# Block attention and a gated product: seven products in 76 of the 80 blocked units, the scans of v at unit ends, and the copy and block sums ahead of tanh in eight units

## The chip, the cores and the metric

One core of a Trainium2 chip. The metric is the device time of one execution in microseconds (us). The engines are named as the profile names them: PE (TensorE matmuls), PEld (its weight loads), DVE (VectorE), ACT (ScalarE), POOL (GpSimd) and SP (SyncE, which issues nearly all DMAs).

## The reference

```python
# attention within chunks of 64 rows, 8 batches x 8 heads x 576 rows, head_dim 64
scores = scale * np.matmul(q_c, k_c.transpose(0, 1, 2, 4, 3))
attn = np.exp(scores - np.max(scores, axis=-1, keepdims=True))
attn = attn / (np.sum(attn, axis=-1, keepdims=True) + 1e-09)
out = np.matmul(attn, v_c)
# its result, as x of 4608 rows by 512, goes through
h = x @ w_in          # 512 x 2048
g = h - np.tanh(h)
return (g @ w_out).astype(np.float32)   # 2048 x 512
```

## The kernel before

The 4608 rows are nine groups of 512. Groups 0 and 1 are computed in a plain way while weights are prepared; groups 2 to 8 go through the class `Fast`. There a group is two halves (b = 0, 1), and a half is eight units (j = 0 to 7). A unit takes two of the sixteen column blocks of `w_in` (j and j + 8) for 256 rows. Its first product gives four 128x128 blocks of h in PSUM (`ph`, two buffers); tanh and a subtraction follow; sums of blocks of the result go, as seven 128x128 operands in two f16 parts each (`gh`, `gl`), through the second product. All matmuls of this stage are f16, three for each operand pair (high*high, low*high, high*low).

From group SEVEN = 4 on x is kept in 2x2 blocks ("blocked"), 5 groups, 10 halves, 80 units. A unit's first product is made there in one of two ways. **Plain** (`gemm1`, L691): 24 matmuls of 256 columns. **Seven products** (`seven`, L706): 42 matmuls of 128 columns, in two parts, P5, P4, P1, P6 (24 matmuls) and P2, P7, P3 (18). Between the two parts ACT copies three blocks of `ph` to SBUF (`kept_back`, L711) and DVE adds them up (`joined`, L715 and L716); the second part accumulates on what `joined` wrote and waits for it. After it DVE adds once more (`completed`, L721). `in_seven` (L955) chooses: before, plain are all units with j = 3, j = 0 to 2 of group 4's first half, and j = 6, 7 of the last half: 15 plain, 65 seven.

The seven products need combined weights (`sums`). They are made once, one j at a time, by `Half.seven` in six POOL operations, two ACT copies and two DVE subtractions (L556), cut into seven steps, which `make_in` puts among the units of groups 2 and 3; they are stored to DRAM (`kept`) and read back two units before use into three rotating places (`load`, L854), except j = 6 and 7, which stay.

The order on every engine is the order of the code in `run`. For unit s of the blocked stage: PE the first part of s; loads; `closing` (DVE `completed` of s - 1); extra work of slot 0; ACT tanh of s - 1 (L725); `kept_back` and `joined` of s; `shrink` of s - 1 (DVE L732, then three POOL lines L733 to L735); `split` of s - 2 (ACT L744, DVE L745); PE the second product of s - 3 (L764), and where that ends a half the output arithmetic of `finish` (three ACT, three POOL, five DVE L777); PE the second part of s; extra work of slot 1. So PE's second part of s stands behind DVE's `joined` of s, and the first part of s behind `shrink` of s - 2, which frees its buffer.

The extra work is the attention of the next group, which `beside` places in the units by hand (key 2 * unit + slot). For each half it falls on the same j:

- j = 3: slot 0 PE weights times values, slot 1 `blocks`: twice ACT L425, L426 and DVE L427, the second round behind the first one's L427
- j = 4: slot 0 `differences` (POOL) and the scan of v, `halves` (DVE L311; in first halves also L313); slot 1 PE scores, more differences, and in second halves six tiny DVE operations of `power_of` (L578 to L583)
- j = 5: slot 0 DVE `largest` (L363); j = 6: slot 0 `shifted`; j = 7: `totals`; j = 0: `divided`; j = 1: the transposes; j = 2: POOL `split_low`

For group 4 itself this lies among the plain units of group 3; its second scan stands at slot 0 of unit 5 there, and PE's `spread` (L290), which reads it, at slot 1 of that unit.

Of the kernel before, what the change touches and what calls it, by code (L numbers as in the profile page):

```python
# [31 lines left out]
FC = DFF // P  # L32
# [3 lines left out]
NG = len(SIZES)  # L36
# [23 lines left out]
def attn_ffn_kernel(ctx: ExitStack, tc: tile.TileContext, qE, kE, vE, qL, kL, vL, w_in, w_out, out):  # L60
# [604 lines left out]
    class Fast:  # L665
# [146 lines left out]
        def run(self, at, before):  # L812
# [50 lines left out]
            for unit in units:  # L863
                s = unit["s"]
                unit["x"] = self.x = xs[unit["g"], unit["b"]]
                if unit["seven"]:
                    unit["sums"] = unit.get("sums") or resident[unit["j"]]
                    unit["ph"] = ps_h.tile([P, 4, P], F32, name="ph")
                    self.seven(unit, ("P5", "P4", "P1", "P6"))
                else:  # L870
                    self.gemm1(unit["b"], unit["j"])
                    unit["ph"] = self.ph
                while loads and loads[0]["s"] <= s + 2:
                    load()
                if pending:
                    closing(pending)
                for f in at.pop(o + 2 * s, []):
                    f()
                t = self.tanh() if pending else None
                if unit["seven"]:  # L880
                    self.kept_back(unit)
                    self.joined(unit)
                last, self.ready = self.ready, None
                if pending:
                    self.ph = pending["ph"]
                    self.shrink(pending["b"], pending["j"], t=t)
                last, self.ready = self.ready, last
                self.split()
                self.ready = last
                if self.stores:  # L890
                    self.stores[0] -= 1
                    if not self.stores[0]:
                        self.stores.pop()()
                        self.stores = None
                if len(self.queue) > (s >= (SEVEN - FAST) * n + 2) and unit is not units[-1]:
                    self.gemm2()
                if unit["seven"]:
                    self.seven(unit, ("P2", "P7", "P3"))
                for f in at.pop(o + 2 * s + 1, []):
                    f()  # L900
                pending = unit
# [51 lines left out]
            store(nc.scalar, 0, left)  # L953

    def in_seven(g, b, j):  # L955
        return j != 3 and (g, b, j // 4) != (SEVEN, 0, 0) and (g, b, j // 6) != (NG - 1, 1, 1)

    def beside(att, at, g):

        o = 2 * FC * (g - FAST)  # L960

        def put(unit, part, f, *args):
            at[o + 2 * unit + part].append(lambda: f(*args))

        put(-4, 0, att.halves, g, 0)
        late = g == SEVEN
        put(4 + late, 0, att.halves, g, 1)
        put(12, 1, lambda: powers.update({g: half.power_of(g)}))
        for b, u in enumerate((3, 11)):
            first = g == SEVEN and not b  # L970
            put(u + 1 + first, 1, att.scores, g, b)
            put(u + 2 + first, 0, att.largest, g, b)
            put(u + 3, 0, att.shifted, g, b)
            put(u + 3, 1, att.exponent, g, b)
            put(u + 4, 0, att.totals, g, b)
            put(u + 5, 0, att.divided, g, b)
            put(u + 5, 1, att.high, g, b)
            put(u + 6, 0, att.transpose, g, b)
            put(u + 6, not first, att.split_high, g, b)
            put(u + 7 - first, first, att.split_low, g, b)  # L980
            put(u + 8, 0, att.values, g, b)
            put(u + 8, 1, att.blocks, g, b)
            put(u + 9, 0, att.differences, g, b, 0)
            put(u + 9, 1, att.differences, g, b, 1)
            put(u + 10, 1, att.rounded_high, g, b, 1)
            put(u + 10, 1, att.rounded_low, g, b, 1)
            put(u + 11, 1, att.rounded_high, g, b, 0)
            put(u + 11, 1, att.rounded_low, g, b, 0)
            if g + 1 < NG:
                for i in range(2):  # L990
                    p = FIRST[g + 1] + 2 * b + i, 2 * b + i
                    put(u + 2 + i, 1, att.load, *p, "q")
                    put(u + 4 + i, 1, att.load, *p, "k")
                    put(u + 7, 1, att.load, *p, "v")
        put(6 - late, late, att.spread, g)
        put(6 - late, 1, att.greatest, g)
# [245 lines left out]

    def make_in(i, j):
        if j not in made_in:
            made_in[j] = half.seven(j, temporary[i % 2] if i else stream[2], stream[i % 2] if j < FC // 2 - 1 else temporary[1], j == FC // 2 - 1)
        next(made_in[j])

    o = 2 * FC * (SEVEN - FAST)
    at[o - 23].append(rooms)
    at[o - 15].append(more_rooms)  # L1250
    steps = [[29 * i // 4 - 22 + k for k in (0, 1, 2, 4, 5, 6, 7)] for i in range(FC // 2 - 1)]
    wanted = [j for j in range(FC // 2) if any(in_seven(g, b, j) for g in range(SEVEN, NG) for b in range(2))]
    for i, j in enumerate(wanted):
        for k in steps[i]:
# [83 lines left out]
```

## Time and profile before

| what | value |
|---|---|
| median of 3 runs | 785.83 us (785.73 to 786.14) |
| the profiled execution's own time | 786.32 us |
| its span, first to last instruction | 784.5 us |
| granted TensorE clock | 1.00 |
| PE busy | 770.5 us, 98% |
| DVE busy | 635.0 us, 81% |
| POOL busy | 502.3 us, 64% |
| ACT busy | 479.5 us, 61% |
| blocked stage, first seven-product unit to end | 396.35 to 784.5 us |

The profile gives for each engine when an instruction began and how long it lasted; a row of the timeline merges neighbours of one kind (x24), and the bracket at its end says how long the engine had stood idle and which instruction ended that. A matmul's end is modelled, so PE's pace is read from starts.

### The profile page before, as it was taken

The numbers are of one execution on the slowest core, as the hardware profiler recorded it, in microseconds if no ns is written. First come the engines' busy times: TensorE is split into PE (matmuls) and PEld (weight loads), VectorE is DVE, ScalarE is ACT, GpSimd is POOL, SyncE is SP. The second block draws the span as 40 slices with busy tenths as digits, with TensorE's granted clock in tenths as the row PEclk, the third lists the DMA queues.
The fourth block names the chain that finished last, engine by engine and source line by source line (L and its number), as shares of the span: only waits on it lengthen the run. The fifth ranks groups of instructions, "written<-read, shape, count | busy, mean of one in ns | idle before, by whom it ended". The sixth has DMA issues, their size and how long they took to land. (4 is left out here: it accounts for less than half of the span.)

```text
span 784.5 us, 23249 instructions
## 1 busy us (share of the span) xinstructions
PE 770.5 (98%) x9839; PEld 662.8 (84%) x9839; DVE 635.0 (81%) x1021; ACT 479.5 (61%) x787; POOL 502.3 (64%) x572
## 2 busy tenths in 40 slices
PE   8999999999999999999999999999999999999997
PEld 4878886666788888888899998999999989999996
DVE  5896998888698887786878887888888888787565
ACT  5877988566466455364556565747565656566443
POOL 1100002586678889689677777777867786878763
PEclk9999999999999999999999999999999999999999
DMA  9854441210233333133363535353534442424110
GB/s 347 315 196 164 162 162 53 81 28 2 81 81 95 82 109 96 42 82 122 82 217 72 198 61 186 83 181 91 164 108 145 125 139 60 131 58 135 55 55 28
DMA packets 74600, 91.68 MB, mean 117 GB/s; under 512 B 34560, under 2 KB 41728, under 8 KB 74496
## 3 DMA queue, kind: packets, MB, share of 16 engines
q1 hardware_dynamic: 74064, 89.55, 37.1%
q8 instruction: 77, 1.26, 0.7%
q10 hardware_dynamic: 432, 0.66, 0.2%
q14 instruction: 27, 0.22, 0.1%
HBM read 70.25 MB, written 12.58 MB: 106 GB/s over the span
## 5 line engine op out<-in xcount | busy, mean ns | idle before, releaser
L733 POOL TENSOR_TENSOR xl<-xl 128x256 f32<-128x256 f32 x111 | 146.5, 1320 | 113.3 <-DVE xl L732 101.4
L725 ACT ACTIVATE t<-ph,sig 128x512 f32<-128x512 f32 x112 | 77.0, 687 | 153.5 <-DVE ph L721 123.3
L691 PE MATMUL ph<-xh,wh 128*128 128x256 f16 x1068 | 123.7, 273 | 1.5 <-DVE xl L732 1.5
L691 PEld LDWEIGHTS <-wh 128*128 128x128 f16 x1068 | 103.4, 98 | 14.3 <-issue 2.2
L732 DVE SCALAR_TENSOR_TENSOR xl<-ph,sig,t 128x512 f32<-128x512 f32 x112 | 83.3, 744 | 27.4 <-ACT t L725 27.2
L706 PE MATMUL ph<-xh,wl 128*128 128x128 f16 x1344 | 97.8, 219 | 0.0
L706 PE MATMUL ph<-xh,wh 128*128 128x128 f16 x1332 | 95.7, 219 | 0.9 <-DVE ph L716 0.8
L764 PEld LDWEIGHTS <-gh 128*128 128x128 f16 x924 | 88.0, 98 | 10.1 <-issue 0.4
L764 PEld LDWEIGHTS <-wl 128*128 128x128 f16 x882 | 85.2, 98 | 9.6
L745 DVE SCALAR_TENSOR_TENSOR gl<-xl,to_g,gh 128x896 f16<-128x896 f32 x68 | 85.4, 1255 | 9.4 <-ACT gh L744 9.4
L764 PE MATMUL po<-wl,gh 128*128 128x256 f16 x610 | 87.7, 273 | 0.2 <-DVE wl L777 0.2
L706 PEld LDWEIGHTS <-wh 128*128 128x128 f16 x1332 | 81.7, 98 | 4.9 <-DVE ph L716 3.6
L735 POOL TENSOR_TENSOR xl<-xl 128x256 f32<-128x256 f32 x111 | 82.7, 745 | 0.0
L764 PE MATMUL po<-wl,wl 128*128 128x256 f16 x549 | 82.1, 273 | 0.0
L706 PEld LDWEIGHTS <-wl 128*128 128x128 f16 x1344 | 81.0, 98 | 0.8
L744 ACT ACTIVATE gh<-xl,to_g 128x896 f16<-128x896 f32 x68 | 71.0, 1045 | 15.3 <-POOL xl L735 14.9
L734 POOL TENSOR_TENSOR xl<-xl 128x128 f32<-128x128 f32 x111 | 67.5, 608 | 0.0
L764 PE MATMUL po<-wh,wl 128*128 128x256 f16 x333 | 59.7, 273 | 0.0
L605 PE MATMUL ph<-xh,wh 128*128 128x512 f16 (+2 forms) x252 | 59.3, 378 | 0.4 <-ACT xh L269 0.4
L745 DVE SCALAR_TENSOR_TENSOR wl<-xl,to_g,wl 128x896 f16<-128x896 f32 x44 | 55.1, 1253 | 5.1 <-ACT wl L744 5.0
L744 ACT ACTIVATE wl<-xl,to_g 128x896 f16<-128x896 f32 x44 | 45.9, 1043 | 15.3 <-POOL xl L735 14.2
L636 PE MATMUL po<-wh,gh 128*128 128x512 f32 x128 | 52.8, 415 | 0.0
(231 smaller groups left out, 1602.2 us busy)
## 6 DMA issues: line engine op xcount, KB each, us to landing
wl<-kept SPq DMA_DIRECT2D x96, 256.0 KB, 3.8
raw<-w_in SPq DMA_DIRECT2D x16, 512.0 KB, 3.8
raw<-w_out SPq DMA_DIRECT2D x16, 512.0 KB, 5.3
xl<-qL SPq DMA_DIRECT2D x28, 256.0 KB, 3.5
rawv<-vL SPq DMA_DIRECT2D x28, 256.0 KB, 3.0
rawk<-kL SPq DMA_DIRECT2D x28, 256.0 KB, 4.6
out<-wl SPq DMA_DIRECT2D x55, 128.0 KB, 2.6
kept<-wl SPq DMA_DIRECT2D x12, 256.0 KB, 2.2
```

The costliest lines, as they stand in the source:

```text
L605: nc.tensor.matmul(ph, lhsT=w[:, kc * P:(kc + 1) * P], rhs=x[b][:, kc, cols], start=(k == 0), stop=(k == 3 * KC - 1))
L636: nc.tensor.matmul(self.po[t], lhsT=gg[a][:, ts], rhs=wt[fc][1][b], start=(fc == 0 and a == b == 0), stop=(fc == FC - 1 and a == 1))
L691: nc.tensor.matmul(self.ph[:, 1 - f::2, :], lhsT=half_w[fc][:, w, kc * P:(kc + 1) * P], rhs=rhs, start=(k == 0), stop=(k == 3 * KC - 1))
L706: nc.tensor.matmul(ph[:, o], lhsT=a[:, w, i * P:(i + 1) * P], rhs=x[v][:, m, i * P:(i + 1) * P], start=(n == "P5" and k == i == 0), stop=( ...
L725: nc.scalar.activation(t, self.ph, AF.Tanh, scale=self.powers[0])
L732: nc.vector.scalar_tensor_tensor(out=u[:, :4], in0=self.ph, scalar=sig, in1=t, op0=ALU.mult, op1=ALU.subtract)
L733: engine.tensor_add(u[:, 4:6], u[:, 1:3], u[:, 0:4:3])
L734: engine.tensor_add(u[:, 6], u[:, 1], u[:, 2])
L735: engine.tensor_sub(u[:, 0:4:3], u[:, 0:2], u[:, 2:4])
L744: nc.scalar.activation(gh, u, AF.Copy, scale=powers[1])
L745: nc.vector.scalar_tensor_tensor(out=gl, in0=u, scalar=powers[1], in1=gh, op0=ALU.mult, op1=ALU.subtract)
L764: nc.tensor.matmul(place[m], lhsT=part[:, self.SUM[m]], rhs=w[m][:, o], start=first, stop=(last and part is gl), skip_group_check=True)
```

## The change

Five edits:

1. `in_seven`: plain remain j = 0, 1 of group 4's first half and j = 6, 7 of the last half. Eleven units change to seven products: j = 2 and 3 of (4, 0) and j = 3 of the nine other halves.
2. An eighth product (j = 3) is therefore made: the steps start every 6.5 half-units instead of 7.25, for eight j's, and the temporaries alternate the other way round.
3. `halves` (scan of v) goes from slot 0 to slot 1 of its unit.
4. Group 4's own second scan goes from slot 0 of unit 5 to slot 1 of unit 2.
5. In units with j = 4, groups 4 to 7, `kept_back` and `joined` come before `closing` and tanh of the unit before.

```diff
+                early = unit["seven"] and unit["j"] == FC // 4 and unit["g"] < NG - 1
+                if early:
+                    self.kept_back(unit)
+                    self.joined(unit)
                 if pending:
                     closing(pending)
                 for f in at.pop(o + 2 * s, []):
                     f()
                 t = self.tanh() if pending else None
-                if unit["seven"]:
+                if unit["seven"] and not early:
                     self.kept_back(unit)
                     self.joined(unit)
...
     def in_seven(g, b, j):
-        return j != 3 and (g, b, j // 4) != (SEVEN, 0, 0) and (g, b, j // 6) != (NG - 1, 1, 1)
+        return (g, b, j // 2) != (SEVEN, 0, 0) and (g, b, j // 6) != (NG - 1, 1, 1)
...
-        put(-4, 0, att.halves, g, 0)
+        put(-4, 1, att.halves, g, 0)
         late = g == SEVEN
-        put(4 + late, 0, att.halves, g, 1)
+        put(4 - 2 * late, 1, att.halves, g, 1)
...
-            made_in[j] = half.seven(j, temporary[i % 2] if i else stream[2], stream[i % 2] if j < FC // 2 - 1 else temporary[1], j == FC // 2 - 1)
+            made_in[j] = half.seven(j, temporary[1 - i % 2] if i else stream[2], stream[i % 2] if j < FC // 2 - 1 else temporary[1], j == FC // 2 - 1)
...
-    steps = [[29 * i // 4 - 22 + k for k in (0, 1, 2, 4, 5, 6, 7)] for i in range(FC // 2 - 1)]
+    steps = [[(13 * i - 43) // 2 + k for k in (0, 1, 2, 4, 5, 6, 7)] for i in range(FC // 2)]
```

## Rows read from the trace of the kernel before

**Rows 1.** The page's first part: span, then busy time and share of each engine.

```profile
span 784.5 us, 23249 instructions
PE 770.5 (98%) x9839; PEld 662.8 (84%) x9839; DVE 635.0 (81%) x1021; ACT 479.5 (61%) x787; POOL 502.3 (64%) x572
```

**Rows 2.** Busy time by stretch: PE, PEld, DVE, ACT, POOL; group 3, then one blocked unit.

```profile
267.00:390.00 123.00, 118.46 (x1502) 105.03 (x1500) 95.37 (x115) 62.08 (x85) 102.29 (x114) 1.00 0.30 88
...
445.88:450.51 4.63, 4.63 (x65) 4.40 (x63) 4.51 (x8) 3.07 (x6) 3.87 (x5) 1.00 1.01 351
```

**Rows 3.** Timeline of PE, units j = 3 to 5 of half (4, 1): start, duration, instruction.

```profile
430.28 2.78 PE L691 MATMUL ph<-xh,wh 128*128 128x256 f16 x24
...
436.21 0.50 PE L706 MATMUL ph<-xh,wl 128*128 128x128 f16 x6
...
437.55 0.38 PE L764 MATMUL po<-wh,wl 128*128 128x256 f16 x2
...
440.03 0.51 PE L706 MATMUL ph<-xh,wh 128*128 128x128 f16 x6
...
442.23 0.51 PE L706 MATMUL ph<-xh,wl 128*128 128x128 f16 x6
...
445.88 0.50 PE L706 MATMUL ph<-xh,wh 128*128 128x128 f16 x6
```

**Rows 4.** Timeline of PE: a wait in group 3, one in (4, 0), one in (5, 0).

```profile
320.40 0.49 PE L290 MATMUL po<-ident,sums 128*128 128x128 f32 x2 [1.33 <-DVE sums L313]
...
385.51 0.71 PE L691 MATMUL ph<-xh,wh 128*128 128x256 f16 x5 [1.52 <-DVE xl L732]
...
480.24 0.51 PE L706 MATMUL ph<-xh,wh 128*128 128x128 f16 x6 [0.28 <-DVE ph L716]
```

**Rows 5.** Timeline of DVE over the same units of (4, 1); last, one row of (5, 0).

```profile
432.18 0.42 DVE L721 TENSOR_TENSOR ph<-ph,t 128x256 f32<-128x256 f32 x1
433.36 0.75 DVE L732 SCALAR_TENSOR_TENSOR xl<-ph,sig,t 128x512 f32<-128x512 f32 x1 [0.76 <-ACT t L725]
434.29 1.57 DVE L745 SCALAR_TENSOR_TENSOR wl<-xl,to_g,wl 128x896 f16<-128x896 f32 x1 [0.18 <-ACT wl L744]
435.79 0.68 DVE L427 SCALAR_TENSOR_TENSOR xh<-psa,xh 128x512 f16<-128x512 f32 x1
437.62 0.69 DVE L427 SCALAR_TENSOR_TENSOR xh<-psa,xh 128x512 f16<-128x512 f32 x1 [1.15 <-ACT wh L426]
438.22 1.21 DVE L311 TENSOR_REDUCE v<-rawv 128x1 f32<-128x1024 f32 x1
439.35 0.29 DVE L715 TENSOR_TENSOR ph<-ph,t 128x128 f32<-128x128 f32 x1
439.67 0.30 DVE L716 TENSOR_TENSOR ph<-ph,t 128x128 f32<-128x128 f32 x1
439.88 0.74 DVE L732 SCALAR_TENSOR_TENSOR xl<-ph,sig,t 128x512 f32<-128x512 f32 x1
440.54 1.14 DVE L745 SCALAR_TENSOR_TENSOR gl<-xl,to_g,gh 128x896 f16<-128x896 f32 x1
...
443.82 1.22 DVE L363 TENSOR_REDUCE mx<-psa 128x16 f32<-128x1024 f32 x1
...
445.43 0.30 DVE L716 TENSOR_TENSOR ph<-ph,t 128x128 f32<-128x128 f32 x1
...
479.43 0.21 DVE L313 TENSOR_SCALAR sums<-v 128x1 f32<-128x1 f32 x1
```

**Rows 6.** Timeline of ACT (tanh, split, copy) and of POOL in the same units.

```profile
432.64 0.69 ACT L725 ACTIVATE t<-ph,sig 128x512 f32<-128x512 f32 x1 [2.73 <-DVE ph L721]
433.23 1.03 ACT L744 ACTIVATE wl<-xl,to_g 128x896 f16<-128x896 f32 x1
...
438.04 0.49 ACT L711 COPY t<-ph 128x384 f32<-128x384 f32 x1
...
440.70 1.56 POOL L733 TENSOR_TENSOR xl<-xl 128x256 f32<-128x256 f32 x1 [1.50 <-DVE xl L732]
```

## The prediction, made before the changed kernel ran

> **What bounds the kernel now.** I read the page first: PE is busy 98% of the span at full clock, DVE 81% [rows 1]. So fewer columns on PE should be time won, if nothing else becomes late. The second view is the busy time by stretch: in an ordinary blocked unit of 4.63 us DVE is busy 4.51 [rows 2]. The share of 81% hides that: DVE has spare time only at j = 0 to 2 and in waits. The third view is PE's timeline: its starts give its pace and the few places where it waits [rows 3, 4]. The last are DVE's and ACT's timelines over units j = 3 to 5, where the change acts [rows 5, 6]. There the reader is to see that from 437.62 to 445.73 DVE runs without a gap, and that its `joined` of unit 5 ends at 445.73, 0.15 us before PE needs it at 445.88. **PE is the bound, with DVE 0.15 us behind it.**
>
> **The change on PE.** A plain unit: 24 matmuls; (2.78 - 0.27) / 23 = 0.109 us each, 2.62 us (0.27 is a single one: 0.38 for two, less 0.109). A seven-product unit: 24 from 436.21 to 437.55, 0.056 each, so 42 take 2.35 us [rows 3]. Eleven units gain 0.27 each, **3.0 us**. The waits that the edits aim at: 0.19 us at j = 4 of second halves (the second product ends at 437.55 + 21 x 0.109 = 439.84, the next part starts at 440.03), 0.44 in first halves (0.28 idle, and 0.16 by which a modelled end overhangs the pace) [rows 3, 4], and 1.5 us (1.33 and the overhang) at `spread` in group 3, which waits for group 4's own scan [rows 4].
>
> The Trainium skill, "TensorE: Matmul & The Clock Gate", section "Back-to-back issue gap", speaks against seven products: it gives some 81 ns per matmul as the sustained pace at 128 columns. An estimate by that page: 42 x 0.081 = 3.40 us a unit, 0.78 more than a plain one, 8.6 us more in eleven. The trace has 56 ns throughout these units and decides.
>
> **The change on DVE, second halves**, walked in (4, 1) from T3 = 430.28, the start of j = 3; every number from [rows 5, 6].
> - `completed`(2) ends at 432.60 and tanh(2) runs 432.64 to 433.33, as before: output arithmetic ahead of them holds DVE.
> - New: the copy of unit 3 follows tanh at 433.23 (now the split starts there) and ends at 433.71; `joined`(3) takes 0.62 (439.35 to 439.97): 433.75 to 434.38. `shrink`(2) starts 0.21 after L716's start: 434.29, was 433.36.
> - `split`(1) at 434.95. It took 1.57 before, having started behind POOL's sums, and 1.14 where it starts ahead of them (440.54; POOL's sum, at 440.70, then takes 1.56). Now it starts ahead: 1.14, upper bound 1.57. First L427 at 436.02, was 435.79. The second is 1.83 behind, as in the rows, since two ACT operations lie between: 437.85 to 438.54.
> - `joined`(4) comes first now: 438.45 to 439.07. PE needs it at 436.21 - 0.27 + 1.34 + 2.29 = 439.57: this wait is gone.
> - New: `completed`(3), 438.98 to 439.40; then tanh(3), which had not waited for DVE while j = 3 was plain, 439.50 to 440.19. DVE has nothing else in its queue and stands still. `shrink`(3) at 440.22 (was 439.88), tanh(3) holds the split on ACT to 441.14, `split`(2) on DVE at 441.17 (was 440.54).
> - From there to `largest` it was 443.82 - 440.54 = 3.28; the scan now stands in between, 1.13 more (438.22 to 439.35): `largest` at 445.58. To the end of `joined`(5) another 1.91 (443.82 to 445.73): 447.49, and PE starts 0.06 later, at **447.55**.
> - PE is due there at 439.57 + 2.20 + 3.65 = 445.42 (440.03 to 442.23, 442.23 to 445.88) [rows 3]. It waits **2.13 us**.
>
> So a second half gains 0.27 + 0.19 and loses 2.13: **+1.67 us**. Bounds: all small latencies and `power_of` uncontended by POOL, +0.8; `split`(1) at 1.57, +2.1. Behind the scan wait `completed`(4), tanh(4), the copy and `joined`(5); none of it can overtake. At j = 6 the delay is over: `shifted` and what follows fill 4.5 us of a unit, as before, and PE was moved as far as DVE.
>
> **First halves** have L313 (0.25 us with its start) but no `power_of`. The same walk, 39.96 later: `split`(2) at 481.13, scan and L313 to 482.51, `completed`(4) and `largest` to 485.13, `joined`(5) at 485.82. PE is due at 485.38: wait 0.50, against 0.27 + 0.44 gained: -0.2 (-0.6 to +0.3).
>
> **The other halves.** (7, 1) has no scan behind it (there is no tenth group): its wait is 2.13 - 1.13 = 1.0, gain 0.27: +0.7. (8, 0) isn't reordered, so its copy of unit 4 waits for `completed`(3) and tanh(3): `joined`(4) ends 438.85 + 0.1 + 0.69 + 0.4 + 0.66 = 440.7 on this clock, PE due 439.57, 1.2 less 0.27: +0.9. (8, 1) has no attention: -0.27. (4, 0) changes two units, 0.54, and has a first half's wait and somewhat more, since DVE starts it late: +0.3 (-0.5 to +1).
>
> Sum of the blocked stage: 3 x 1.67 - 3 x 0.2 + 0.7 + 0.9 - 0.27 + 0.3 = **+6.0 us**.
>
> **Group 3 and the eighth product.** The product adds six POOL operations, two ACT copies and two DVE subtractions, each of 0.7 to 1.6 us (an estimate from the subtraction L427 and the sum L733) [rows 5, 6]; two stores; and 22 reads, two more for each of eleven units. SP issues the reads two units ahead, some 9 us, and they wait only for the matmuls that read their place last, which by then are done; I cost them at nothing, and if one came late PE would wait its part. POOL is 83% busy in this group (102.29 of 123) and DVE 78% [rows 2], so the product mostly fills gaps. `spread`'s 1.5 us is won at unit 5, since the scan is then two units old. But the group ends at 385.51 in a wait of 1.7 us for `shrink` of unit 0 [rows 4]: there DVE is late, not PE, and the last product's subtractions now come 1.5 units later, nearer to it. What PE won earlier is largely given back in that wait. Between -2.5 (all kept) and +1.5 (two more subtractions on the late chain) I take **-0.7**, nearer to the loss of the gain than to its keeping, since L732 ended that wait.
>
> Total +5.3. On the profiled execution's 786.32 that is 791.6; it stands 0.5 above the median, 785.83, so I forecast **791.1 us** for the median.
>
> **Rivals.**
> - *The DVE chain holds* (ends faster). If j = 5 isn't late, 3.0 of columns, three waits each of 0.44 and 0.19 (1.9) and up to 1.5 of `spread` are won: 785.8 - 6.3 = 779.5. For it: PE is 98% busy, and every edit takes DVE work from in front of a named wait. Against: 0.15 us of slack at `joined`(5), where the walk adds 1.76. It decides at 445.88: were `joined`(5) to end by 445.4, it would be right. Chance 0.20.
> - *Half of it*: the 3.28 us between `split`(2) and `largest`, tiny operations beside POOL's sums for the most part, shrink by 1 where POOL lies otherwise; the wait is near 1 us in second halves, and the blocked stage and `spread` together break even: 785 to 787. Chance 0.11.
> - *Late entry*: the eighth product delays POOL's sums and DVE at the end of group 3 by 2 to 4 us, on top of the forecast: 795. For it: the wait at 385.51 is there already. Chance 0.08.
> - The rule of the Trainium skill's page above on 128 columns: as a mechanism, PE's pace falls in the eleven units when both parts are seven-product. By that page's figure the time would be 791.1 + 3.0 + 8.6 = 803; 65 units at 56 ns leave it a chance of 0.01.
> - The forecast itself: 0.60, own range 787.5 to 794.5.
>
> **Numbers.** The bounds of the terms (second halves 3 x 0.8 to 3 x 2.1, first halves -1.8 to +0.9, group 3 -2.5 to +1.5) make the forecast's own range. To hold eight in ten the range reaches down into the faster case and half-way: 782 to 795. A difference under 0.2%, 1.6 us, is about what a measurement can't tell from no change. Faster: the first rival and a little of the second, 0.22; within it 0.10; slower 0.68.
>
> **What would show it.** Right: in second halves of groups 4 to 6 PE's second part at j = 5 waits some 2 us for DVE L716, and DVE is without a gap from `shrink`(3) to `joined`(5) with L311 in it; j = 4 waits for nothing; first halves shorter by some tenths, second halves longer by 1.5 us or so; PE L706 at 56 ns in 76 units; `spread` no longer waits for L313, and the wait for L732 at the end of group 3 is longer. Wrong: `joined`(5) in time, or L311 elsewhere in DVE's order, or halves all shorter than before.

## The result, and the profile after

The changed kernel takes **794.08 us** (median; 794.02 to 794.26), beside 785.83 (785.69 to 786.18) for the kernel before on the same chip: a ratio of 1.0104, 95% interval 1.009 to 1.0119. It is slower by 8.2 us, where +5.3 was forecast. The profiled execution took 794.08 us as well, so it stands at its median; that of before stood 0.5 above its own, and from profile to profile the difference is 7.8.

The first part of the page of the changed kernel:

```profile
span 792.1 us, 23760 instructions
PE 768.9 (97%) x10037; PEld 662.9 (84%) x10037; DVE 645.7 (82%) x1056; ACT 484.1 (61%) x800; POOL 510.0 (64%) x578
```

PE's busy time fell from 770.5 to 768.9 us and the span grew by 7.6 [rows 1]: columns were won, and more than that was lost in waits. Only 1.6 of the 3.0 us of columns show in the busy time, because the modelled end of the last matmul ahead of each new wait is counted as busy (0.16 us each; an estimate, about nine new waits). The waits of PE over the whole span (engine, what waited, for what: us in total, times, longest):

```profile
PE ph L706 <- DVE ph L716: 9.9, 10, 1.7
...
PE ph L706 <- DVE xl L732: 1.8, 1, 1.8
PE po L764 <- DVE wl L777: 1.2, 3, 0.7
```

The first line is most of the case. Ten times PE's second part stood idle for DVE's `joined`, 9.9 us; with the 0.16 by which a modelled end overhangs the pace, 11.5. The timeline of PE of the changed kernel over units j = 3 to 5 of (4, 1) has one of the ten:

```profile
430.51 0.50 PE L706 MATMUL ph<-xh,wh 128*128 128x128 f16 x6
...
436.16 0.50 PE L706 MATMUL ph<-xh,wh 128*128 128x128 f16 x6
...
438.50 0.38 PE L764 MATMUL po<-wh,wl 128*128 128x256 f16 x2
...
440.80 0.50 PE L706 MATMUL ph<-xh,wh 128*128 128x128 f16 x6
...
442.99 0.51 PE L706 MATMUL ph<-xh,wl 128*128 128x128 f16 x6
...
448.50 0.51 PE L706 MATMUL ph<-xh,wh 128*128 128x128 f16 x6 [1.70 <-DVE ph L716]
```

j = 3 is in seven products now: from 430.51 run the second part of j = 2 and behind it, without a break, the first part of j = 3, and from 436.16 the second part of j = 3 and the first of j = 4. The second part of j = 4 starts without a bracket (440.80), and that of j = 5 stands behind an idle time of 1.70 us (448.50): 1.87 with the overhang. Counted in matmuls of 56 ns, the first part of j = 3, which the prediction calls T3, starts 18 of them after 430.51, at 431.51: 1.23 later than the 430.28 of the prediction's clock. The timeline of DVE of the changed kernel over the same units tells why:

```profile
433.42 0.42 DVE L721 TENSOR_TENSOR ph<-ph,t 128x256 f32<-128x256 f32 x1
...
436.16 1.14 DVE L745 SCALAR_TENSOR_TENSOR wl<-xl,to_g,wl 128x896 f16<-128x896 f32 x1
...
440.19 0.42 DVE L721 TENSOR_TENSOR ph<-ph,t 128x256 f32<-128x256 f32 x1
441.43 0.75 DVE L732 SCALAR_TENSOR_TENSOR xl<-ph,sig,t 128x512 f32<-128x512 f32 x1 [0.81 <-ACT t L725]
442.36 1.57 DVE L745 SCALAR_TENSOR_TENSOR gl<-xl,to_g,gh 128x896 f16<-128x896 f32 x1 [0.18 <-ACT gh L744]
443.86 0.41 DVE L578 TENSOR_TENSOR sig<-from,from_w 128x1 f32<-128x1 f32 x1
...
444.75 0.20 DVE L582 TENSOR_TENSOR undo_g<-undo_g,from_w 128x1 f32<-128x1 f32 x1
...
445.07 1.22 DVE L311 TENSOR_REDUCE v<-rawv 128x1 f32<-128x1024 f32 x1
446.20 0.42 DVE L721 TENSOR_TENSOR ph<-ph,t 128x256 f32<-128x256 f32 x1
446.54 1.21 DVE L363 TENSOR_REDUCE mx<-psa 128x16 f32<-128x1024 f32 x1
...
448.14 0.30 DVE L716 TENSOR_TENSOR ph<-ph,t 128x128 f32<-128x128 f32 x1
```

The scan L311 stands where it was moved to (445.07), ahead of `completed` (446.20), `largest` and `joined` of unit 5, whose L716 PE waits for. In front of it DVE stands still for 0.81 us (441.43), until ACT's tanh is done; before, the scan ended ahead of these steps [rows 5]. From 442.36 to 448.44 DVE has no gap to catch up in.

The waits of the other halves, from PE's timeline of the changed kernel: `joined` in (4, 0), (5, 0), (7, 1), (8, 0) and (8, 1).

```profile
406.90 0.51 PE L706 MATMUL ph<-xh,wh 128*128 128x128 f16 x6 [1.09 <-DVE ph L716]
...
488.83 0.28 PE L706 MATMUL ph<-xh,wh 128*128 128x128 f16 x2 [0.73 <-DVE ph L716]
...
693.13 0.23 PE L706 MATMUL ph<-xh,wh 128*128 128x128 f16 x1 [0.56 <-DVE ph L716]
...
727.90 0.28 PE L706 MATMUL ph<-xh,wh 128*128 128x128 f16 x2 [0.99 <-DVE ph L716]
...
760.85 0.34 PE L706 MATMUL ph<-xh,wh 128*128 128x128 f16 x3 [0.32 <-DVE ph L716]
```

With the overhang, and less the 0.27 won in columns and the old wait of the half, the ten come to this:

| half | wait forecast | wait measured | net forecast | net measured |
|---|---|---|---|---|
| (4,1), (5,1), (6,1) | 2.13 | 1.87, 1.87, 1.51 | +1.67 each | +1.4, +1.4, +1.05 |
| (5,0), (6,0), (7,0) | 0.50 | 0.89 each | -0.2 each | +0.2 each |
| (4,0) | "somewhat more" than 0.50 | 1.25 | +0.3 | +0.7 |
| (7,1) | 1.0 | 0.72 | +0.7 | +0.45 |
| (8,0), at j = 4 | 1.2 | 1.16 | +0.9 | +0.9 |
| (8,1), at j = 3 | none | 0.48 | -0.27 | +0.2 |

The net values sum to +6.7. The 1.51 of (6, 1) is smaller because PE had already stood 0.35 us inside its second product at 599.27. The stretches say the same (columns as in [rows 2]; the last three are the granted clock, the busy share of DMA and its GB/s): group 3, then from j = 5 of (4, 1) to j = 5 of (5, 0), and from there to j = 5 of (5, 1).

```profile
267.00:390.00 123.00, 117.72 (x1509) 104.38 (x1507) 97.68 (x118) 63.75 (x88) 108.75 (x120) 1.00 0.34 100
442.99:484.30 41.31, 39.61 (x671) 36.95 (x665) 34.93 (x63) 24.73 (x37) 30.47 (x35) 1.00 0.47 142
484.30:524.92 40.62, 39.89 (x671) 37.18 (x667) 34.23 (x62) 24.66 (x37) 30.44 (x35) 1.00 0.50 144
```

The last two took 40.21 and 40.07 before: +1.10 and +0.55.

**Group 3.** POOL and DVE are busier in it, 108.75 and 97.68 us for 102.29 and 95.37 [rows 2]. PE's timeline of the changed kernel there:

```profile
309.00 0.81 PE L764 MATMUL po<-wl,gh 128*128 128x256 f16 x6 [0.70 <-DVE wl L777]
...
320.21 1.16 PE L351 MATMUL psa<-rawk,xl 64*64 64x64 f32 x64 [1.41 <-issue]
...
385.90 0.27 PE L706 MATMUL ph<-xh,wl 128*128 128x128 f16 x2 [1.85 <-DVE xl L732]
```

The wait of `spread` is gone, and so is one of 0.36 at 349.07. New ones stand at 307.70 to 309.00 and at 320.21 (0.45 and 0.87, 1.57 with the overhang). That at 358.22 (1.20) isn't new: before, it stood at 358.16 with 1.48. The one at the end of the group has grown by 0.33. ACT's timeline of the same kernel shows where the new ones come from:

```profile
305.56 0.62 ACT L564 CAST wl<-wh 128x512 f16<-128x512 f32 x1 [1.81 <-POOL wh L548]
306.09 0.68 ACT L779 ACTIVATE wl<-po,undo_g 128x512 f32<-128x512 f32 x1
...
317.18 0.62 ACT L560 CAST wl<-wh 128x512 f16<-128x512 f32 x1 [0.45 <-POOL wh L545]
317.71 1.08 ACT L412 ACTIVATE xh<-psa 128x512 f16<-128x512 f32 x2
```

L560 and L564 are the copies of a made product, held up by POOL's L545 and L548; behind them in ACT's queue stand the output arithmetic (L779) that DVE's L777 and then PE wait for, and L412, which DVE's L414 (318.82 to 320.11) and, behind that, the scores at 320.21 need. (That is read from the order: the bracket of the scores names no engine.) Unit 2 of the blocked stage starts at 385.90 against 385.51 [rows 4], though ahead of group 3 this execution ran 0.54 us earlier than that of before: the group costs +0.9. By the same count the waits of the group add up to 6.1 us, where before they were 5.2.

So: blocked stage +7.4 (776.05 - 385.90 against 768.27 - 385.51, starts of the last plain unit and of unit 2), group 3 +0.9, the start of the span -0.5: +7.8. (The -0.5 is mostly a difference between executions: those of experiments 2, 3 and 7, with the same code up to there, reached group 3 at 266.38 to 266.45, this one at 266.13, that of before at 266.67.)

### The profile page after: what moved, and what is told of

Read it like the earlier page. It is cut to its first block, busy times and chain, and to the rows that moved or that the text cites. A ratio compares the mean times of both kernels' runs of the same rounds, so it can differ in the third digit from the quotient of the medians.

```text
span 792.1 us, 23760 instructions
## 1 busy us (share of the span) xinstructions
PE 768.9 (97%) x10037; PEld 662.9 (84%) x10037; DVE 645.7 (82%) x1056; ACT 484.1 (61%) x800; POOL 510.0 (64%) x578
## 4 chain that ended last, share of the span: by engine, by line
PE 58%; DVE 21%; POOL 8%; ACT 7%; issue 5%; DMA 1%; POOLq 0%; ACTq 0%; DVEq 0%
PE ph L706 17%; PE po L764 15%; PE po L636 10%; PE ph L605 9%; DVE gl L745 2%; PE ph L691 2%; DVE wl L745 2%; DVE xl L732 2%; POOL xl L733 2%; ACT t L711 1%; PE ph L1106 1%; POOL xl L735 1%; DVE v L311 1%; PE psa L186 1%; PE psa L351 1%
## 5 line engine op out<-in xcount | busy, mean ns | idle before, releaser
L733 POOL TENSOR_TENSOR xl<-xl 128x256 f32<-128x256 f32 x111 | 142.6, 1285 | 119.5 <-DVE xl L732 101.7
L706 PE MATMUL ph<-xh,wh 128*128 128x128 f16 x1530 | 110.4, 219 | 9.9 <-DVE ph L716 9.9
L706 PE MATMUL ph<-xh,wl 128*128 128x128 f16 x1608 | 114.7, 219 | 1.8 <-DVE xl L732 1.8
L706 PEld LDWEIGHTS <-wh 128*128 128x128 f16 x1530 | 93.5, 98 | 15.8 <-DVE ph L716 14.5
L732 DVE SCALAR_TENSOR_TENSOR xl<-ph,sig,t 128x512 f32<-128x512 f32 x112 | 83.2, 743 | 21.9 <-ACT t L725 21.7
L706 PEld LDWEIGHTS <-wl 128*128 128x128 f16 x1608 | 95.9, 98 | 2.6 <-issue 2.0
L745 DVE SCALAR_TENSOR_TENSOR gl<-xl,to_g,gh 128x896 f16<-128x896 f32 x68 | 87.5, 1287 | 8.8 <-ACT gh L744 8.6
L764 PEld LDWEIGHTS <-wl 128*128 128x128 f16 x882 | 85.2, 98 | 9.5
L691 PE MATMUL ph<-xh,wh 128*128 128x256 f16 x804 | 93.1, 273 | 0.0
L691 PEld LDWEIGHTS <-wh 128*128 128x128 f16 x804 | 78.0, 98 | 9.7 <-issue 0.5
L735 POOL TENSOR_TENSOR xl<-xl 128x256 f32<-128x256 f32 x111 | 84.2, 759 | 0.0
L734 POOL TENSOR_TENSOR xl<-xl 128x128 f32<-128x128 f32 x111 | 73.3, 660 | 0.0
L715 DVE TENSOR_TENSOR ph<-ph,t 128x128 f32<-128x128 f32 x76 | 22.6, 297 | 40.8 <-ACT t L711 39.9
```

The source lines that it names most:

```text
L691: nc.tensor.matmul(self.ph[:, 1 - f::2, :], lhsT=half_w[fc][:, w, kc * P:(kc + 1) * P], rhs=rhs, start=(k == 0), stop=(k == 3 * KC - 1))
L706: nc.tensor.matmul(ph[:, o], lhsT=a[:, w, i * P:(i + 1) * P], rhs=x[v][:, m, i * P:(i + 1) * P], start=(n == "P5" and k == i == 0), stop=( ...
L732: nc.vector.scalar_tensor_tensor(out=u[:, :4], in0=self.ph, scalar=sig, in1=t, op0=ALU.mult, op1=ALU.subtract)
L733: engine.tensor_add(u[:, 4:6], u[:, 1:3], u[:, 0:4:3])
L734: engine.tensor_add(u[:, 6], u[:, 1], u[:, 2])
L735: engine.tensor_sub(u[:, 0:4:3], u[:, 0:2], u[:, 2:4])
```

## Experiments

All ratios are against the kernel before in the same series of runs on one chip, with 95% intervals; edits are against the changed kernel, except where said.

**1. The scans back in slot 0 of j = 4**, group 4's early one kept.

```diff
-        put(-4, 1, att.halves, g, 0)
+        put(-4, 0, att.halves, g, 0)
-        put(4 - 2 * late, 1, att.halves, g, 1)
+        put(4 - 2 * late, int(late), att.halves, g, 1)
```

> Theory A (the DVE chain: in units j = 3 to 5 DVE's instructions stand in one order, and what lies in that order ahead of joined of unit 5 delays PE one for one). With the scan back in slot 0 it stands behind completed(3), where DVE stood idle 0.81 us for tanh(3); split(2) can't start before 442.36 on the changed kernel's clock anyway, since it waits for ACT. So the scan's 1.13 us (1.38 with L313) goes out of the chain: the wait at j = 5 falls from 1.87 to some 0.7 in second halves and from 0.89 to about 0 in first ones. Three of each, and 1.25 in (4, 0): 794.1 - 7.3 = 786.8 us. Rival B (the new units themselves cost: 22 more reads, 42 matmuls in two parts, j = 3 no longer a rest for ACT): the scan's place moves the wait from j = 5 to j = 4, 794 within 1 us. Rival C (the eighth product in group 3): no change, 794.

787.21 us, ratio 1.0016 (1.0006 to 1.0025): of the 8.2 us, 6.9 go with the place of the scan alone. DVE's timeline of this kernel in (4, 1):

```profile
438.88 0.42 DVE L721 TENSOR_TENSOR ph<-ph,t 128x256 f32<-128x256 f32 x1
439.21 1.21 DVE L311 TENSOR_REDUCE v<-rawv 128x1 f32<-128x1024 f32 x1
440.34 0.74 DVE L732 SCALAR_TENSOR_TENSOR xl<-ph,sig,t 128x512 f32<-128x512 f32 x1
441.05 1.15 DVE L745 SCALAR_TENSOR_TENSOR gl<-xl,to_g,gh 128x896 f16<-128x896 f32 x1
...
445.94 0.30 DVE L716 TENSOR_TENSOR ph<-ph,t 128x128 f32<-128x128 f32 x1
```

The scan runs while ACT does tanh, in the time in which DVE stood idle. From `completed` to L716 it is 7.06 us (438.88 to 445.94), where it was 7.95 in the changed kernel: 0.89 less. The second halves' waits are 0.98, 0.97 and 0.96, and those of (4, 0) and of the first halves are gone. In this order the rest of the change all but breaks even.

**2. `joined` behind tanh again in the units with j = 4.**

```diff
-                early = unit["seven"] and unit["j"] == FC // 4 and unit["g"] < NG - 1
+                early = False
```

> Theory A: without the early copy and sums, joined(4) comes behind completed(3), tanh(3) and the copy, 1.9 us later than now, and PE's second part of unit 4 waits 1.1 us for it. But split(2), the scan, largest and joined(5) keep their times, so PE reaches j = 5 later by what it waits less there: 794 within 0.7 us; the waits are 1.1 at j = 4 and 0.8 at j = 5 where now 1.87 stands at j = 5; first halves lose some 0.3 each. Rival B: the reordering is what keeps j = 4 in time, so undoing it costs 1.1 us in each of eight halves, 802 us. Rival D (the reordering itself is the harm, since it holds tanh(3) back): 786 to 788.

796.83 us, ratio 1.0135 (1.012 to 1.015), 2.1 us above the upper end expected. The wait at j = 4 came as expected, but that at j = 5 stayed longer. Both, in PE's timeline of this kernel in (4, 1):

```profile
442.52 0.40 PE L706 MATMUL ph<-xh,wh 128*128 128x128 f16 x4 [1.00 <-DVE ph L716]
...
449.42 0.40 PE L706 MATMUL ph<-xh,wh 128*128 128x128 f16 x4 [0.89 <-DVE ph L716]
```

1.16 and 1.06, in place of one of 1.87. I had taken the sum to be nearly the same; here L578 and L582 took 0.69 and 0.60 us again, as before, instead of 0.41 and 0.20. The first halves wait 1.16 at j = 4 in place of 0.89 at j = 5, as expected, (4, 0) 1.52 for 1.25 and (7, 1) 1.16 for 0.72; my own sum had left these out. Together they make some 2.5 of the 2.7 us that the reordering is worth beside the scans in slot 1.

**3. `power_of` moved** from slot 1 of j = 4 to slot 0 of j = 2 (group 4's own stays).

```diff
-        put(12, 1, lambda: powers.update({g: half.power_of(g)}))
+        put(*((12, 1) if late else (10, 0)), lambda: powers.update({g: half.power_of(g)}))
```

> The changed kernel with the six small operations of power_of in slot 0 of j = 2 of second halves in place of slot 1 of j = 4, and nothing else. They take 1.3 us of DVE between split(2) and joined(5) there. Theory A (what stands in DVE's order ahead of joined(5) delays PE one for one, whatever it is): waits of second halves at j = 5 fall by 1.2 to 1.3 each and that of (7, 1) by all of its 0.72, first halves as they are: 794.1 - 3 x 1.25 - 0.7 = 789.6 us. If scan or reordering alone were the cause: no change.

790.27 us, ratio 1.0049 (1.0034 to 1.0064). The second halves' waits fall from 1.87, 1.87 and 1.51 to 0.66, 0.67 and 0.54, the first halves', which have no `power_of`, stay at 0.91, and (7, 1) waits no more. In PE's timeline of this kernel the wait of (4, 1) is

```profile
447.73 0.34 PE L706 MATMUL ph<-xh,wh 128*128 128x128 f16 x3 [0.50 <-DVE ph L716]
```

Six operations on 128x1 hold DVE for 1.2 us, and what leaves DVE's queue there leaves PE's wait.

**4. The eleven units without any reordering**: `early` off, all scans as before.

```diff
-                early = unit["seven"] and unit["j"] == FC // 4 and unit["g"] < NG - 1
+                early = False
-        put(-4, 1, att.halves, g, 0)
+        put(-4, 0, att.halves, g, 0)
-        put(4 - 2 * late, 1, att.halves, g, 1)
+        put(4 + late, 0, att.halves, g, 1)
```

> The changed kernel with seven products in the eleven units and the eighth made product, but none of the reorderings: scans in slot 0 of j = 4 and of group 4's unit 5, copy and sums behind tanh. Theory A: joined(4) ends 1.2 us after PE is due, in every half with attention; joined(5) is then in time. Each second half +0.74 against before, first halves +0.5, (7, 1) and (8, 0) +0.9, (4, 0) +0.6, group 3 as in the changed kernel: 785.8 + 6.2 = 792 (790 to 793.5), so the reorderings as made cost some 2 us and the columns' gain is lost with or without them. Rival C (the eighth product): the loss stands in group 3, with the blocked stage no longer than before. Rival D: 783, the columns' gain.

797.1 us, ratio 1.014 (1.0125 to 1.0155), 5 us above what I expected. In the blocked halves it was about as expected: 1.07 to 1.25 at j = 4 from (4, 1) to (8, 0), with 1.60 in (4, 0) and 0.48 in (8, 1). Most of the miss, 3.4 us, lies in group 3, where `spread` waits 3.0 us and PE then runs slowly. The scan that `spread` needs stands at 321.48 on DVE, behind L414 and a made product's L556, which the ACT copies hold up here as in the changed kernel. PE's timeline of this kernel there:

```profile
322.99 0.55 PE L290 MATMUL po<-ident,sums 128*128 128x128 f32 x2 [2.80 <-DVE sums L313]
323.33 4.43 PE L691 MATMUL ph<-xh,wh 128*128 128x256 f16 x24
```

and the stretch behind the wait (columns as in [rows 2]):

```profile
323.30:326.70 3.40, 3.40 (x18) 2.44 (x17) 1.37 (x5) 0.00 (x0) 1.04 (x1) 0.50 0.27 87
```

24 matmuls took 4.43 us where they take 2.78 [rows 3], at a granted clock of 0.50. Unit 2 of the blocked stage starts at 389.30, 3.4 later than in the changed kernel. So the eleven units and the eighth product alone lose more than the whole change does, but it is group 4's early scan that makes the difference. The blocked stage itself (start of unit 2 to start of the last plain unit) takes 389.6 us here and 390.2 in the changed kernel: the two reorderings there, as made, buy nothing together.

**5. The order alone**, on the kernel before: j = 3 plain, seven made products, group 4's scan at unit 5.

```diff
-        return (g, b, j // 2) != (SEVEN, 0, 0) and (g, b, j // 6) != (NG - 1, 1, 1)
+        return j != 3 and (g, b, j // 4) != (SEVEN, 0, 0) and (g, b, j // 6) != (NG - 1, 1, 1)
-        put(4 - 2 * late, 1, att.halves, g, 1)
+        put(4 + late, int(not late), att.halves, g, 1)
...
-    steps = [[(13 * i - 43) // 2 + k for k in (0, 1, 2, 4, 5, 6, 7)] for i in range(FC // 2)]
+    steps = [[29 * i // 4 - 22 + k for k in (0, 1, 2, 4, 5, 6, 7)] for i in range(FC // 2 - 1)]
```

> The kernel before with the two reorderings alone (scan in slot 1 of j = 4, copy and sums ahead of tanh), j = 3 plain, seven made products. Theory A: no completed(3), no joined(3), tanh(3) free: joined(5) ends near 446.2 on the clock of before's (4, 1), PE due at 445.7, a wait of 0.5 in second halves in place of 0.19, none in first halves in place of 0.44; three of each: 785.8 + 1.1 - 1.3, that is 785 to 786.5. Rival D (the reorderings are the harm): slower than before by 5 us or more, 791. Rival B or C: faster than before by the removed waits, 784.

784.96 us, ratio 0.9986 (0.9976 to 0.9995), just better than expected. With j = 3 plain, the second halves wait 0.30 at j = 5 and the first halves nowhere. The two edits hurt each other: the new order costs nothing beside plain units, the seven products cost most beside the new place of the scan. The length of the blocked stage, against 382.8 before, says it by parts:

| kernel | j = 3 | scan | `joined` of j = 4 | blocked stage |
|---|---|---|---|---|
| experiment 5 | plain | slot 1 | ahead of tanh | -1.2 |
| experiment 1 | seven | slot 0 | ahead of tanh | +0.4 |
| experiment 4 | seven | slot 0 | behind tanh | +6.8 |
| changed kernel | seven | slot 1 | ahead of tanh | +7.4 |
| experiment 2 | seven | slot 1 | behind tanh | +9.9 |

Beside the scan in slot 0, `joined` ahead of tanh wins 6.4 us; the scan's move takes 7.0 away again.

**6. Group 4's early scan alone**, on the kernel before (edit against it):

```diff
-        put(4 + late, 0, att.halves, g, 1)
+        put(4 - 2 * late, int(late), att.halves, g, 1)
```

> The kernel before with one edit alone: group 4's own second scan in slot 1 of unit 2 of group 3. View 1 (what PE wins at spread is given back in the later waits of group 3, since DVE and not PE sets their ends): the wait of 1.5 us at spread is gone, the first product of unit 2 of the blocked stage still starts within 0.4 us of 385.5, the whole at 785.4 to 786. View 2 (won for good): 784.3, the blocked stage 1.5 us earlier.

784.54 us, ratio 0.9979 (0.997 to 0.9989). PE's timeline of this kernel at `spread` and at unit 2 of the blocked stage:

```profile
318.75 0.49 PE L290 MATMUL po<-ident,sums 128*128 128x128 f32 x2
...
383.48 0.38 PE L691 MATMUL ph<-xh,wh 128*128 128x256 f16 x2 [1.54 <-DVE xl L732]
```

`spread` starts 1.65 earlier without a wait, the wait at the end of the group is as long as it was (1.52 before), and unit 2 starts at 383.48 instead of 385.51. This execution reached group 3 0.24 us earlier (266.43 for 266.67), so 1.8 of the 2.0 belong to the edit: the 1.5 of `spread` and the wait at 349.07, which is gone too. What PE won at `spread` was kept: DVE's chain to L732 moved forward with it.

**7. No reads for j = 3**: these units use the sums of j = 7, which stay in SBUF; the eighth product is made as in the changed kernel.

```diff
-            loads = [u for u in units if u["seven"] and u["j"] != FC // 2 - 1]
+            loads = [u for u in units if u["seven"] and u["j"] not in (3, FC // 2 - 1)]
...
-                    unit["sums"] = unit.get("sums") or resident[unit["j"]]
+                    unit["sums"] = unit.get("sums") or resident[unit["j"] if unit["j"] != 3 else FC // 2 - 1]
```

> The changed kernel without the reads of the combined weights of j = 3: its third, sixth and seventh products take those of j = 7, which are in SBUF, so the output leaves out the true ones; all instructions else are the same, with 20 reads of 256 KB less. Theory A: the reads are hidden, 794 within 0.5 us. Rival B (the reads delay the transposes, or PE waits for them): 2 us or more less.

794.35 us, ratio 1.0101 (1.0086 to 1.0116), with 98 reads of 256 KB instead of 118 and the same waits in the halves (1.90 in (4, 1), 0.91 in (5, 0)). The reads cost nothing, as the prediction had them.

**8. What stands ahead of the waits, moved**: the scans in slot 0 (the first in j = 2 from group 6 on), `power_of` as in 3, `early` also in group 8 (in (8, 1) at j = 3).

```diff
-                early = unit["seven"] and unit["j"] == FC // 4 and unit["g"] < NG - 1
+                early = unit["seven"] and unit["j"] == FC // 4 - ((unit["g"], unit["b"]) == (NG - 1, 1))
-        put(-4, 1, att.halves, g, 0)
+        put(*((-4, 0) if g <= SEVEN + 1 else (2, 0)), att.halves, g, 0)
-        put(4 - 2 * late, 1, att.halves, g, 1)
-        put(12, 1, lambda: powers.update({g: half.power_of(g)}))
+        put(4 - 2 * late, int(late), att.halves, g, 1)
+        put(*((12, 1) if late else (10, 0)), lambda: powers.update({g: half.power_of(g)}))
```

> The changed kernel with the scans of groups 5 to 8 out of slot 1 of j = 4 (the first one of a group in slot 0 of j = 2, for group 5 in its old slot 0; the second in its old slot 0 of j = 4), the six small operations of power_of in slot 0 of j = 2, and copy and sums ahead of tanh in (8, 0) too and at j = 3 of (8, 1). Theory A: between shrink(3) and joined(5) then stand only split(2), completed(4) and largest, so that joined(5) ends 0.5 us before PE is due in all halves: against the run with the scan in slot 0 (787.2) the waits of 0.98, 0.97, 0.96, 0.73, 1.17 and 0.48 go: 781.9 us, faster than the kernel before by 0.5%. Rival B (the new units cost in themselves): not under 786.

783.29 us, ratio 0.9966 (0.9953 to 0.9979). No wait for `joined` above 0.2 us is left in the halves of groups 5 to 7; in group 3 all but that of 0.45 at 307.70 are left. The time is 1.4 above what I expected: the blocked stage is 4.3 us shorter than in experiment 1, not 5.3 (a wait of 0.54 for `shrink` in (8, 0), at 718.02, is new; the rest I could not place), and this execution reached group 3 0.5 us later.

**9. The same, and the made products' steps as they were**, the eighth in what room is left at the end.

```diff
-    steps = [[(13 * i - 43) // 2 + k for k in (0, 1, 2, 4, 5, 6, 7)] for i in range(FC // 2)]
+    steps = [[i + k for k in (0, 1, 2, 4, 5, 6, 7)] for i in (-22, -15, -8, -1, 6, 12, 18, 24)]
```

> The kernel with the moved scans and eight made products, whose first four start where they started before (half-units -22, -15, -8, -1) and the rest every six. View P (the eighth product's cost in group 3 is that an ACT copy of a step waits for POOL's sums and holds the output arithmetic behind it): with the fourth product one half-unit later that copy stands elsewhere, the 0.2 and 0.87 us that PE waited for L777 near 308 go, and the other waits of the group stay: 783.3 - 1 = 782.2. View Q (POOL and DVE have simply more to do there, and any order costs it): 783.3 within 0.5 us, the wait turning up elsewhere in the group.

782.32 us, ratio 0.9946 (0.9934 to 0.9959). The waits around 308 and 320 are gone, and that of 1.2 at 358 is down to 0.54, but that at the end of group 3 grew from 2.0 to 3.4. The time is the one expected by view P (782.2), partly by luck: against experiment 8, unit 2 starts 2.1 us earlier, counted from the start of group 3, where 1 us was expected, and the blocked stage behind it takes 1.3 longer (380.2 for 378.9), because the clock fell. PE's timeline of this kernel there, and the stretch behind:

```profile
384.18 0.80 PE L706 MATMUL ph<-xh,wl 128*128 128x128 f16 x6 [3.24 <-DVE xl L732]
```

```profile
384.20:387.00 2.80, 2.80 (x26) 2.73 (x26) 0.00 (x0) 1.37 (x3) 2.79 (x4) 0.50 0.98 187
```

**10. The moves of 8 with j = 3 plain** and seven made products on the old steps: what the moves do without the eleven units. The edits are those of 8, and `in_seven`, temporaries and steps as in 5, with units j = 2 and 3 of (4, 0) plain.

> The same moved scans, group 4's early scan and copy ahead of tanh, but j = 3 plain and j = 0 to 3 of (4, 0) plain as before, and seven made products. It has the waits gone (1.9 us at j = 4, 1.5 at spread) and neither the columns' gain (3.0) nor the eighth product: 784.5 - 1.9 = 782.6 us. Theory A with the eighth product at 2.4 us in group 3 and 1.2 us of waits left in the run with the moved scans: the two are within 1 us of each other, so that eleven more units of seven products are worth nothing by themselves here. If the columns' gain were there in full: 785.3 or more.

782.07 us, ratio 0.9944 (0.9931 to 0.9958): level with 9. Its waits in group 3 are 1.48 (355.91) and 1.70 (383.28), against 0.54 and 3.4 and a slow clock in 9: there the late end of the group, and the clock behind it, take what the eleven units save in columns.

**11. Kernel 9, and the attention's last steps of group 4's second half later** (rounding a unit, transposes half a unit), behind the `shrink` that frees PE's buffer.

```diff
-            put(u + 5, 1, att.high, g, b)
-            put(u + 6, 0, att.transpose, g, b)
+            handed = g == SEVEN and b
+            put(u + 5 + handed, 1, att.high, g, b)
+            put(u + 6, handed, att.transpose, g, b)
```

> The run with the first four steps as before, and group 4's second half at the hand-over to the blocked stage a slot or two later: its rounding (high) from slot 1 of unit 0 to slot 1 of unit 1, its difference and transposes (DVE L394) from slot 0 to slot 1 of unit 1. Then tanh of unit 0 follows the split on ACT and shrink of unit 0 (L732) comes 1.2 us earlier on DVE, in front of L394. Theory A: PE's wait at unit 2 falls from 3.4 us to 2.2, and if the clock then keeps its full level, as it did behind waits of 2.0 us in the other runs, the 1.3 us go too that 24 matmuls lost at half clock (2.41 us in place of 1.28, and the start of the next part): 782.3 - 2.5 = 779.8; with the clock still falling 781.1. If the end of group 3 is set by POOL or by the transposes: 782 within 0.5 us.

**779.91 us**, ratio 0.9925 (0.9913 to 0.9938), the lowest median of all: 5.9 us under the kernel before and 14.2 under the changed one. In DVE's timeline of this kernel `shrink` now comes ahead of L394, which it stood behind in kernel 9 (L394 at 382.25, L732 at 383.39):

```profile
382.05 0.74 DVE L732 SCALAR_TENSOR_TENSOR xl<-ph,sig,t 128x512 f32<-128x512 f32 x1
382.71 1.21 DVE L394 TENSOR_TENSOR a<-psa,a 128x1024 f16<-128x1024 f32 x1
```

PE's timeline has a wait of 2.01 (2.17 with the overhang) in place of 3.24, and the stretch behind it the full clock:

```profile
382.84 0.49 PE L706 MATMUL ph<-xh,wl 128*128 128x128 f16 x6 [2.01 <-DVE xl L732]
```

```profile
384.20:387.00 2.80, 2.80 (x34) 2.57 (x32) 1.73 (x4) 2.80 (x7) 2.80 (x3) 1.00 0.85 146
```

**12. Kernel 10 with the same edit.**

> The same at the hand-over in the kernel with moved scans and j = 3 plain. PE's wait of 1.7 us there falls to 0.5 and the clock was full anyway: 782.1 - 1.2 = 780.9 us. Against the run before it in this call this shows what the eleven units are worth once the waits are gone: columns 3.0 us less, an eighth product in group 3 more.

780.62 us, ratio 0.9936 (0.9923 to 0.995). Its wait at the end of group 3 is 0.45 us. The two intervals overlap; by the medians the eleven units are worth 0.7 us, and the order of the work the rest. PE's timelines of the two add up to about that: of 3.0 us of columns, 1.7 stay in that wait (2.17 against 0.45) and 0.9 in small ones of (8, 0) and (8, 1), and 0.8 are won back in the wait ahead of the scores at 355 (0.73 against 1.49).

## Why the prediction was right, and where it was off

**The case.** The forecast's own case came, by its mechanism: `joined`(5) is late, DVE runs without a gap up to it with L311 in its queue, j = 4 waits for nothing in second halves, and the wait stands at j = 5 for L716. Experiment 1 settles that it is the scan, and experiment 3 that the six small operations in that queue do the same. The first rival (the DVE chain holds) falls with the ten waits; so does the second, since the waits of second halves are not near 1 us. Of the third (late entry) a part came: group 3 cost 1.6 us more than the forecast had it, though mostly in its middle, and its last wait grew by only 0.33. The time, 794.08, lies in the range and 3 us above the forecast: the sum was mis-sized, as follows. That it came this near is in part luck, for the misses on the second halves (-1.1 us in all) and on the first (+1.1) cancel. The own range of the forecast, 787.5 to 794.5, is also narrower than its terms allow: their bounds, simply added up, give 785.5 to 796.1.

**Second halves, "+1.67".** Measured +1.4, +1.4 and +1.05. `split`(1) was taken at 1.14 and took 1.14 (436.16). `split`(2) was also taken at 1.14, by the 3.28 us that the rows had from there to `largest`, and took 1.57; but `power_of`'s L578 and L582 took 0.41 and 0.20 for 0.69 and 0.60, which nearly makes up for it. The walk itself held: with 1.23 added for the later T3, it has `split`(1) at 436.18 and PE at 448.78, and they came at 436.16 and 448.50.

**First halves, "-0.2": this step failed.** They came out at +0.2, three times 0.4 us. They have no `power_of` to make up for it, and the value of 1.14 for `split`(2) was the wrong row. (The 482.51 of that walk is a slip as well: scan and L313 end by it at 483.57. The 485.13 behind it is right.) DVE's timeline of the changed kernel in (5, 0):

```profile
483.66 1.57 DVE L745 SCALAR_TENSOR_TENSOR wl<-xl,to_g,wl 128x896 f16<-128x896 f32 x1 [0.18 <-ACT wl L744]
```

It waits 0.18 us for ACT, and in that time POOL's sum begins (483.56). POOL's timeline of the changed kernel beside the two splits of (4, 1):

```profile
436.32 1.56 POOL L733 TENSOR_TENSOR xl<-xl 128x256 f32<-128x256 f32 x1 [1.04 <-DVE xl L732]
...
442.26 0.72 POOL L733 TENSOR_TENSOR xl<-xl 128x256 f32<-128x256 f32 x1 [1.63 <-DVE xl L732]
```

Where the split starts first (436.16), it takes 1.14 and POOL's sum 1.56; where the sum starts first (442.26, split at 442.36), the sum takes 0.72 and the split 1.57. The prediction had this rule from the rows and applied it to `split`(1), not to `split`(2), for which its own walk had `shrink` at 440.22, ACT's part done at 441.14 and so POOL's sum ahead of the split.

The Trainium skill, "SBUF — State Buffer", section "Who interferes with whom", states such a rule: a DVE instruction with two SBUF inputs and a GpSimd instruction that reads SBUF contend for a shared read interface, and issue order decides who blocks. Both splits have two SBUF inputs, and these four rows agree; so does `shrink` L732, whose one input is in PSUM, at 0.74 or 0.75 throughout.

**The other halves.** (8, 0) came as walked, 1.16 for 1.2, (7, 1) at 0.72 for 1.0. (4, 0) was entered at a loss of 0.3 and cost 0.7. (8, 1) was entered at -0.27, because it has no attention, and waits 0.48 at j = 3: its `joined` stands behind `completed` and tanh of unit 2 and the output arithmetic ahead of them, as in every half, but elsewhere the attention's weights times values hold PE for 0.9 us there (432.95 to 433.86 in (4, 1)), and here PE comes without it. Experiment 8 put `joined` ahead of tanh in this unit, and the wait fell to 0.19. (4, 0) and (8, 1) add 0.9 to the sum. Of the blocked stage's +7.4, 0.7 us stand outside these ten waits; 0.35 of it is the stop at 599.27, and the rest I could not place.

**Group 3, "-0.7: what PE won earlier is largely given back in that wait". This step failed most**, by 1.6 us (+0.9 measured). Both halves of it were wrong. Experiment 6 shows `spread`'s gain kept, 1.8 us at the start of unit 2, counted from the start of group 3. The eighth product then costs 2.7 us by the same count (119.77 for 117.05), of which the move of group 4's first scan makes 0.1 (experiment 1). The prediction had bounded it at +1.5, for two subtractions on DVE. The price came on ACT and POOL instead: with steps every 6.5 half-units a made product's ACT copies wait for POOL's sums, and the output arithmetic and the scores stand behind them. Experiment 9 brought the first four steps back, and the two waits of the middle of the group went; of the 3.1 us that the waits there lost in all, 1.4 came back in a longer wait at its end. So the fear of giving back in that wait was right in part, for another gain than that of `spread`.

**Columns and reads.** The 18 matmuls of j = 3's second part and the 24 of j = 4's first part run from 436.16 to 438.50, 42 in 2.34 us: 56 ns each. The Trainium skill's figure of 81 ns (the page and section that the prediction cites) does not hold here in the 76 units. The reads, costed at nothing, cost nothing (experiment 7).

**The median.** 0.5 us of the 2.9 by which the forecast was short is that of before's profiled execution over its own median, while the profiled execution after is at its own.

## What to carry to other kernels

When the bound engine waits on a second, in-order engine that is busy 4.5 of 4.6 us in the units that matter, count what stands ahead of the awaited instruction in that engine's queue: 1.2 us of scan, or six tiny operations, came out as a wait almost one to one here (0.9 of the scan's 1.1 us, 1.2 of 1.2), whatever the share of busy time over the span says. Put such work where that engine stands still anyway; the 0.8 us beside tanh took most of the scan for nothing. And cost one more step of a filler chain on every queue it passes: here I had costed the eighth product on DVE, and it held up output arithmetic through ACT.

## What the runs showed that I had not expected

A wait of PE can cost more than its length. Behind idle times of 2.80 us (experiment 4) and 3.24 us (experiment 9), each in a stretch in which PE had otherwise been busy, the granted clock stood at 0.50, the 1.2 GHz level, over the whole stretches shown; 24 matmuls of 256 columns took 4.43 us instead of 2.78. Behind 1.85 us (the changed kernel, the line below) and 2.01 us (experiment 11) it stayed at 1.00.

```profile
385.90:389.00 3.10, 3.10 (x41) 2.91 (x41) 1.02 (x3) 2.89 (x5) 3.08 (x4) 1.00 1.00 202
```

Kernels 9 and 11 differ by the one edit shown: 1.2 us of wait, and 2.6 us of span (780.4 and 777.8); by their ratios the time differs by 1.7. The single executions show why these differ. Three of the five of kernel 11, the profiled one among them, have a mean granted clock of 0.999 or 1.00 and took 779.48 to 779.91 us; the other two have 0.997 and 0.998 and took 781.41 and 780.97. Of kernel 9 it is one of five that has 1.00, and it took 781.24; the others took 782.24 to 782.61. So the same kernel can lose the clock in one execution and keep it in the next. Behind which wait it fell in those that have no trace isn't shown, and no length can be read from these four waits below which it is safe.

The Trainium skill, "TensorE: Matmul & The Clock Gate", section "HAM oscillation — how this bites in real kernels", tells of a kernel in which the waits between short stretches of work bring the clock down again each time. Here it was a single wait in a long stretch of work, and it did so in two of these four traces.
